# Batch 2's local q and k: from transposes on TensorE to DMA transposes with ordering copies on VectorE

## The chip, the cores and the metric

One core of a Trainium2 chip runs the kernel. The metric is the time of one execution on the device, in microseconds; a run's time is compared with runs of the kernel before. Engines are named as in the profile: PE (TensorE), DVE (VectorE), ACT (ScalarE), POOL (GpSimd) and SP (SyncE, which here only issues DMAs). DMAs are issued by POOL (loads from memory, which also change float32 to bfloat16) and by SP (stores and DMA transposes).

## The reference

Eight batches, eight heads, 576 positions, head size 64. Heads 0 to 3 attend locally (the last 32 positions), heads 4 to 7 attend to positions at a stride of 32. The attention's output feeds a two-layer network with a squared relu:

```python
scores = scale * np.matmul(q, k.transpose(0, 1, 3, 2))
mask_local = (rel >= 0) & (rel < stride)
mask_strided = (rel >= 0) & (pos[None, :] % stride == pos[:, None] % stride)
...
attn = softmax over the masked scores; attn_out = np.matmul(attn, v)
x = attn_out.transpose(0, 2, 1, 3).reshape(B * S, H * D)
h = x @ w_in          # 4608 x 512 by 512 x 2048
g = np.maximum(h, 0.0) ** 2
out = g @ w_out       # 4608 x 2048 by 2048 x 512
```

## The kernel before

The network is computed in nine chunks of 512 tokens. A chunk has 16 groups of the first product (`mm1`, line 848: four matmuls each, then a relu on ACT into one of four buffers `r`, then one step later a square on DVE into `g`) and 16 groups of the second (`mm2`, line 951: four matmuls each; after every fourth group of an output tile ACT copies the result and SP stores it). All groups are numbered 0 to 287 and put out in order; groups 32 to 47 are chunk 1's first product, 48 to 63 its second one, and group 64 is the first that needs batch 2's attention output. The last two chunks (`SEVEN`) replace the second product by seven smaller products of sums (`mm2_7`, line 915), for which `squares` (line 889) makes sums of the squares on DVE and a copy on POOL. In these two chunks the tiles of the first product come in the order 0, 8, 1, 9, ... 7, 15, and the sums for tile ff are made when ff is 8 or more.

The attention of the batches is woven between these groups. The table `PLAN` says ahead of which group a step is put out: the line `38: C3k G2+0+1+2+4+5+6` puts these steps ahead of group 38. There is no other planner: every engine and every queue executes what it is given in the order in which the program puts it out, so a step's place in the table is its place on every engine that it uses. A helper `later(n, fn)` puts work out n groups later.

Heads are handled in pairs; a pair of one batch is a "unit". Units 8 and 9 are the local pairs of batch 2, units 12 and 13 those of batch 3. The steps that the change touches:

- `l2k8+9`, `l2q8+9` (line 287): POOL loads k or q of both units, six positions to a row, into a part of `xt` that is still free. They stand in groups 6 and 12 and stay there.
- `c8kv` (line 300): a cast step, a reordering copy of unit 8's k on DVE from that place into a tile `k_l` of 96 rows.
- `T8kv` (line 487): six transposes on PE of 96x96 into a PSUM bank, then one copy on DVE (last letter `v`) or ACT (`a`) that evicts and puts the positions in order, into `kTl` (k) or `qT` (q).
- `A12k` (line 390): one DMA transpose, issued by SP, of the tile `k_l` into a spare part: for k, two further on among the four `kTl` buffers; for q, a tile `qT`.
- `R12kv` (line 397): a copy on DVE or ACT that puts the positions in order, from that spare part to `kTl` or a new `qT`. `A` and `R` together do what `T` does; batch 3 uses them already.
- `X2k`, `X2q` (line 358): DMA transposes of the strided heads' k and q, issued by SP. `C3k`, `C3q` (line 352): POOL loads the next batch's, into the tiles that X2k and X2q read.
- `G2+0+1+2+4+5+6` (line 580): local scores of units 8 and 9: 24 matmuls, unit 8's twelve first, into six PSUM banks; ACT takes exponentials of each bank (the numbers are the groups by which each is put off), DVE multiplies with the mask.
- `D8.0`, `D8.1` (line 807): exponentials times v for the first and second head of unit 8, then a division on DVE; `E8` (line 825): a DMA transpose, issued by SP, of unit 8's output into `xt`, which `mm1` reads.
- `H2v` (line 448): a copy on DVE of parts of v; `U3` (line 417): loads of v; `s2`, `x2+3` (lines 672, 700): scores and output of the strided heads; `k21v` (line 367): a copy on DVE of their k; `x1.0` to `x1.2` and `E5a`: the end of batch 1.

Of the kernel before, what the change touches and what calls it, by code (L numbers as in the profile page):

```python
# [40 lines left out]
21: s1.1 D5.0  # L41
22: l3k12+13 s1.2 U2
23: E4a D5.1
24: x1.0
26: X2k l3q12+13 x1.1 X2q
28: E5a x1.2
29: c8kv
30: c8qv
31: c9kv c9qv
33: T8kv  # L50
34: C3q T8qv
35: T9qa
36: H2v T9kv
38: C3k G2+0+1+2+4+5+6
39: c12kv A12k
40: c13kv A13k
43: D8.0
44: c12qv A12q
45: k21v c13qv A13q D9.0
47: U3 D8.1  # L60
48: Q16k D9.1 E8
49: E9
50: Q17q Q16q s2
52: Q17k
55: X3k X3q
56: C4k C4q x2+3
# [73 lines left out]
def kernel(  # L140
# [332 lines left out]
    def later(n, fn, key=None):  # L473
        pending.append((clock[0] + n, key, fn))
# [369 lines left out]
    gs = {}  # L844
# [3 lines left out]
    def mm1(c, ff, kks=range(4), order=range(4), pool=None):  # L848
        if c not in gs:
            gs[c] = g_pool.tile([128, 16, 512], BF16, name="g_sb")  # L850
        g = gs[c]
        if kks[0] == order[0]:
            phs[ff] = bank(pool or "ph")
        ph = phs[ff]
        for kk in kks:
            nc.tensor.matmul(ph, w_in_tile(kk, ff),  # L856
                             xt[kk][:, 512 * c:512 * (c + 1)],
                             start=(kk == order[0]), stop=(kk == order[-1]))
        if kks[-1] != order[-1]:
            return  # L860
        r = r_pool.tile([128, 512], BF16, name="r")
        nc.scalar.activation(r, ph, AF.Relu)  # L862
        if c in SEVEN:
            later(1, lambda: squares(c, ff, r))
            return
        later(1, lambda: nc.vector.tensor_tensor(g[:, ff, :], r, r, op=ALU.mult))  # L866
# [20 lines left out]
        nc.vector.tensor_tensor(t[nm], x, y, op=ALU.subtract)  # L887

    def squares(c, ff, r):
        g, i = gs[c], ff % 8  # L890
        if not ss:
            att.close()
            late = ctx.enter_context(tc.tile_pool(name="sums", bufs=1, reuse_waits="tile"))
            for nm in ("1", "2", "3", "4", "a"):
                ss[nm] = late.tile([128, 8, 2, 128], mybir.dt.float32r, name=f"s{nm}")
        nc.vector.tensor_tensor(g[:, ff, :], r, r, op=ALU.mult)  # L896
        if ff < 8:
            return
        S = {k: x[:, i] for k, x in ss.items()}
        a1, a2 = (g[:, k, :].rearrange("p (u t c) -> p u t c", u=2, t=2) for k in (i, ff))  # L900
        nc.gpsimd.tensor_copy(S["a"], a2[:, :, 1])  # L901
        nc.vector.tensor_tensor(S["1"], a1[:, :, 1], a2[:, :, 1], op=ALU.add)
        nc.vector.tensor_tensor(S["2"], S["1"], a1[:, :, 0], op=ALU.subtract)
        last = lambda: nc.vector.tensor_tensor(S["4"], a2[:, :, 0], S["2"], op=ALU.subtract)
        later(15 + (4, 4, 5, 6, 7, 8, 9, 10)[i] - 2 * i, last)
        if i < 7:
            return
        for k in range(0, 8, 4):
            a1 = g[:, k:k + 4, :].rearrange("p k (u t c) -> p (k u) t c", u=2, t=2)
            nc.vector.tensor_tensor(ss["3"][:, k:k + 4].rearrange("p k u c -> p (k u) c"), a1[:, :, 0], a1[:, :, 1],  # L910
                                    op=ALU.subtract)
# [298 lines left out]
```

## Time and profile before

| | us |
|---|---|
| median of three runs | 295.23 (294.79 to 295.24) |
| the profiled execution | 295.08 |
| its span, first to last instruction | 293.4 |
| PE busy | 287.2 (98%) |
| DVE busy | 199.9 (68%) |
| ACT busy | 167.0 (57%) |
| POOL busy | 86.7 (30%) |

Rows of the order of instructions give the start in us from the span's start, the length in us, the engine, the line, the operation, output <- input, the shape, and in brackets how long the engine sat idle before and what ended that. SPq and POOLq are the engines' queues of DMA issues; the length of such a row is the length of the issue, not of the transfer. Rows of the chain of waits give start, length, and the work on the chain that ended last. Rows of DMA issues end with the time from issue to landing. PEld is the loading of weights into PE, which overlaps the matmuls.

### The profile page before, as it was taken

The page shows a single profiled execution, that of the slowest core. Times are in us where ns is not written, and L with a number is a line of the kernel's source. Part 1 is how long each engine was busy: PE and PEld are TensorE (multiplying, and loading weights), DVE is VectorE, ACT ScalarE, POOL GpSimd, SP SyncE. Part 2 cuts the span into 40 slices and gives each one's busy share as a digit, 9 for nine tenths or more (in the row PEclk, how much of TensorE's full clock was granted, in tenths as well). Part 3 has the DMA queues.
Part 4 walks back from the last instruction along what each step waited for, and adds up shares of the span by engine and source line. Part 5 has one row for each costly group of instructions (what it writes and reads, how often), then busy time and mean ns, then how long its engine had stood idle before and what let it go on. Part 6 is the DMA issues. An engine that isn't in the chain of part 4 may idle for free.

```text
span 293.4 us, 6453 instructions
## 1 busy us (share of the span) xinstructions
PE 287.2 (98%) x2506; PEld 152.5 (52%) x2506; DVE 199.9 (68%) x489; ACT 167.0 (57%) x306; POOL 86.7 (30%) x135
## 2 busy tenths in 40 slices
PE   7999999999999999999999999999999999999995
PEld 3554555544444454544445444444444444984594
DVE  5666797776366746866366826673389979968983
ACT  3767846674657644764567446654676367306610
POOL 8974552062343047074303720000000013102300
PEclk9999999999999999999999999999999999999999
DMA  7999999999999999999998997411001200020003
GB/s 151 180 210 207 199 201 181 171 246 107 185 218 165 129 190 212 152 135 179 179 141 115 178 169 147 84 56 74 36 22 38 93 36 0 2 107 37 2 1 143
DMA packets 91470, 37.23 MB, mean 127 GB/s; under 512 B 77668, under 2 KB 84226, under 8 KB 91440
## 3 DMA queue, kind: packets, MB, share of 16 engines
q0 software_dynamic: 50352, 18.14, 55.6%
q1 hardware_dynamic: 40944, 18.62, 31.2%
q8 instruction: 19, 0.31, 0.4%
q14 instruction: 11, 0.09, 0.1%
q10 hardware_dynamic: 144, 0.07, 0.1%
HBM read 36.83 MB, written 9.44 MB: 158 GB/s over the span
## 4 chain that ended last, share of the span: by engine, by line
PE 96%; DMA 2%; DVE 0%; issue 0%; DVEq 0%; POOLq 0%
PE psb L856 43%; PE psb L962 33%; PE psb L932 9%; DMA w_out_b<-in_q_dram 2%; PE psb L815 2%; PE psb L589 1%; PE psb L544 1%; PE psb L492 1%; PE psb L743 1%; PE psb L680 1%; PE psb L748 1%; PE psb L514 1%; PE psb L337 0%; PE psb L837 0%; PE psb L327 0%
## 5 line engine op out<-in xcount | busy, mean ns | idle before, releaser
L856 PE MATMUL psb<-xt,w_in 128*128 128x512 bf16 x576 | 131.6, 379 | 0.0
L862 ACT ACTIVATE r<-psb 128x512 bf16<-128x512 f32 x144 | 85.6, 599 | 45.6 <-PE psb L856 42.5
L962 PE MATMUL psb<-w_out_b,g_sb 128*128 128x512 bf16 x448 | 101.0, 379 | 0.0
L856 PEld LDWEIGHTS <-w_in 128*128 128x128 bf16 x576 | 53.8, 98 | 60.3 <-issue 0.5
L866 DVE TENSOR_TENSOR g_sb<-r 128x512 bf16<-128x512 bf16 x112 | 47.0, 423 | 43.8 <-ACT r L862 42.6
L962 PEld LDWEIGHTS <-g_sb 128*128 128x128 bf16 x448 | 42.0, 98 | 47.6
L966 ACT COPY y<-psb 128x512 f32<-128x512 f32 x28 | 16.5, 589 | 42.6 <-PE psb L962 42.5
L901 POOL CAST sa<-g_sb 128x256 fp32r<-128x256 bf16 x16 | 9.7, 603 | 98.1 <-DVE g_sb L896 98.1
L725 DVE TENSOR_TENSOR xt<-psb,rv 64x288 bf16<-64x288 f32 x36 | 17.3, 479 | 14.3 <-ACT rv L713 13.9
L599 ACT ACTIVATE e<-psb 128x384 bf16<-128x384 f32 x36 | 15.5, 505 | 2.8 <-PE psb L589 2.8
L821 DVE TENSOR_TENSOR x_l<-psb,rinv 96x384 bf16<-96x384 f32 x28 | 15.5, 554 | 1.0
L596 DVE TENSOR_TENSOR e<-e,mask_all 128x576 bf16<-128x576 bf16 x24 | 10.0, 454 | 8.8 <-ACT e L599 8.6
L896 DVE TENSOR_TENSOR g_sb<-r 128x512 bf16<-128x512 bf16 x32 | 13.0, 419 | 3.3 <-ACT r L862 3.3
L355 POOL DMA_DIRECT2D q_t<-in_q_dram x6 | 3.4, 568 | 38.0 <-DMA qT_s<-q_t 35.9
L284 POOL DMA_DIRECT2D q_l<-in_q_dram x16 | 11.6, 729 | 8.1 <-DMA v_s<-in_v_dram 3.7
L284 POOL DMA_DIRECT2D k_l<-in_k_dram x16 | 11.7, 735 | 1.7 <-issue 0.9
L932 PE MATMUL psb<-t,s 128*128 128x256 f32 x96 | 12.2, 283 | 0.0
L718 DVE TENSOR_TENSOR xt<-psb,rv 64x162 bf16<-64x162 f32 x24 | 11.2, 469 | 1.2 <-ACT rv L713 0.5
L932 PEld LDWEIGHTS psb<-t,s 128*128 128x128 f32 x96 | 11.6, 189 | 0.0
L355 POOL DMA_DIRECT2D k_t<-in_k_dram x6 | 3.2, 536 | 27.3 <-DMA kT_s<-k_t 25.9
L944 DVE TENSOR_TENSOR y<-psb,y 128x256 f32<-128x256 f32 x19 | 8.0, 423 | 4.3 <-PE psb L932 3.5
L443 POOL DMA_DIRECT2D vl<-in_v_dram x8 | 9.8, 1226 | 3.8 <-DVE xt L718 2.9
(153 smaller groups left out, 303.4 us busy)
## 6 DMA issues: line engine op xcount, KB each, us to landing
out_dram<-y SPq DMA_DIRECT2D x35, 256.0 KB, 2.7
vl<-in_v_dram POOLq DMA_DIRECT2D x8, 288.0 KB, 8.2
w_out_b<-in_moe_w_out_dram POOLq DMA_DIRECT2D x4, 512.0 KB, 14.7
q_t<-in_q_dram POOLq DMA_DIRECT2D x7, 288.0 KB, 6.3
k_t<-in_k_dram POOLq DMA_DIRECT2D x7, 288.0 KB, 7.2
w_in<-in_moe_w_in_dram POOLq DMA_DIRECT2D x2, 768.0 KB, 13.5
v_s<-in_v_dram POOLq DMA_DIRECT2D x12, 108.0 KB, 7.7
k_l<-in_k_dram POOLq DMA_DIRECT2D x16, 72.0 KB, 7.5
```

The source lines that it names most:

```text
L284: nc.gpsimd.dma_start(out=t[:, :, hh, :], in_=src[b, 2 * p + hh].rearrange("(t p) d -> p t d", p=QL))
L599: nc.scalar.activation(e[:, row, 4 * QL * i:4 * QL * (i + 1)], bk[row][i][:, 0:4 * QL], AF.Exp, scale=scale)
L718: nc.vector.tensor_tensor(t, po[half(par), f].rearrange("c (a g m) -> c g m a", a=n, g=3), rv[half(par), w * f:w * (f + 1)].rearrange("c ( ...
L725: nc.vector.tensor_tensor(to[:, :, :, :, par], po[half(par)].rearrange("c f (a h m) -> c h m f a", a=n, h=3)[:, h], rv[half(par)].rearrang ...
L821: nc.vector.tensor_tensor(x, po[0:QL, :, 0:D], rinv[0:QL].to_broadcast([QL, NL, D]), op=ALU.mult)
L856: nc.tensor.matmul(ph, w_in_tile(kk, ff), xt[kk][:, 512 * c:512 * (c + 1)], start=(kk == order[0]), stop=(kk == order[-1]))
L862: nc.scalar.activation(r, ph, AF.Relu)
L866: later(1, lambda: nc.vector.tensor_tensor(g[:, ff, :], r, r, op=ALU.mult))
L896: nc.vector.tensor_tensor(g[:, ff, :], r, r, op=ALU.mult)
L932: nc.tensor.matmul(pa, a, b, start=k == 0 and n not in "273", stop=k == 7, skip_group_check=True)
L962: nc.tensor.matmul(py, g[:, ff, 128 * j:128 * (j + 1)], w_out_b[:, ff, :], start=(ff == 0), stop=(ff == 15))
L966: nc.scalar.copy(y, py)
```

## The change

Two parts. First, `T8kv`, `T8qv`, `T9qa` and `T9kv` (24 transposes on PE, three evictions on DVE and one on ACT) go. In their place stand `A8k`, `A9k`, `A8q`, `A9q` (four DMA transposes on SP) and `R8kv`, `R9kv`, `R8qv`, `R9qv` (four ordering copies on DVE). The casts move from groups 29 to 31 to groups 24 (k) and 28 (q), directly ahead of their DMA transposes; X2k and X2q move from group 26 to 29, so that on SP they stand behind the four new transposes. G2 moves from group 38 to 40, D8.0 from 43 to 44, D9.0 from 45 to 46, D8.1 from 47 to 48, D9.1 from 48 to 49, E9 from 49 to 50; E8 follows D9.1, from 48 to 49.

Second, in the two `SEVEN` chunks the sums for ff 14, until now put out directly behind its square, are put out two groups later, by a new function `sums`: behind the square of ff 7 and ahead of that of ff 15. The last difference of ff 14 (`last`) keeps its place.

```diff
-24: x1.0
-26: X2k l3q12+13 x1.1 X2q
-28: E5a x1.2
-29: c8kv
-30: c8qv
-31: c9kv c9qv
-33: T8kv
-34: C3q T8qv
-35: T9qa
-36: H2v T9kv
-38: C3k G2+0+1+2+4+5+6
-39: c12kv A12k
-40: c13kv A13k
-43: D8.0
-44: c12qv A12q
-45: k21v c13qv A13q D9.0
-47: U3 D8.1
-48: Q16k D9.1 E8
-49: E9
-50: Q17q Q16q s2
+24: c8kv c9kv A8k A9k x1.0
+26: l3q12+13 x1.1
+28: E5a x1.2 c8qv c9qv A8q A9q
+29: X2k X2q
+34: C3q
+35: R8kv
+36: H2v R9kv
+38: C3k R8qv
+39: c12kv A12k R9qv
+40: c13kv A13k G2+0+1+2+4+5+6
+44: c12qv A12q D8.0
+45: k21v c13qv A13q
+46: D9.0
+47: U3
+48: Q16k D8.1
+49: D9.1 E8
+50: Q17q Q16q s2 E9
...
     def squares(c, ff, r):
...
         nc.vector.tensor_tensor(g[:, ff, :], r, r, op=ALU.mult)
-        if ff < 8:
-            return
+        if ff == 14:
+            later(2, lambda: sums(g, ff))
+        elif ff > 7:
+            sums(g, ff)
+
+    def sums(g, ff):
+        i = ff % 8
         S = {k: x[:, i] for k, x in ss.items()}
         a1, a2 = (g[:, k, :].rearrange("p (u t c) -> p u t c", u=2, t=2) for k in (i, ff))
         nc.gpsimd.tensor_copy(S["a"], a2[:, :, 1])
         nc.vector.tensor_tensor(S["1"], a1[:, :, 1], a2[:, :, 1], op=ALU.add)
         nc.vector.tensor_tensor(S["2"], S["1"], a1[:, :, 0], op=ALU.subtract)
         last = lambda: nc.vector.tensor_tensor(S["4"], a2[:, :, 0], S["2"], op=ALU.subtract)
-        later(15 + (4, 4, 5, 6, 7, 8, 9, 10)[i] - 2 * i, last)
+        later(15 + (4, 4, 5, 6, 7, 8, 7, 10)[i] - 2 * i, last)
```

More of the change, by code (lines that the diff above doesn't have):

```diff
@@ L889, in squares @@
     def squares(c, ff, r):
-        g, i = gs[c], ff % 8
+        g = gs[c]
         if not ss:
```

## The prediction

> **What bounds the kernel now.** I read the page, then the chain of waits, then the order of instructions on VectorE (DVE) and on the queues around the change, then the issues of DMAs. The page first:
>
> ```profile
> PE 287.2 (98%) x2506; PEld 152.5 (52%) x2506; DVE 199.9 (68%) x489; ACT 167.0 (57%) x306; POOL 86.7 (30%) x135
> DMA  7999999999999999999998997411001200020003
> PE 96%; DMA 2%; DVE 0%; issue 0%; DVEq 0%; POOLq 0%
> ```
>
> TensorE (PE) carries 96% of the chain, so anything taken off PE shortens the run, and any wait put before it lengthens it by its whole length. The DMA engines have no free slice until two thirds of the span. The chain at the place of the change (start, length, work; "L492 x6" is one of the four steps of transposes on PE that go, the first and the last of them shown, "L589 x24" the local scores of batch 2):
>
> ```profile
> 52.38 0.26 PE psb L492 x6
> 52.64 0.86 PE psb L856 x4
> ...
> 55.74 0.26 PE psb L492 x6
> 57.73 0.77 PE psb L589 x24
> 58.50 4.42 PE psb L856 x20
> ...
> 83.22 6.91 PE psb L856 x32
> ...
> 97.63 0.62 PE psb L589 x24
> ```
>
> PE runs without a hole. A group of the large matmuls takes 0.86. The scores take 0.77 here and 0.62 for batch 4: the first lost 0.15 to T9kv, whose eviction ends at 58.02 (DVE row 57.28 below).
>
> **What goes.** Four times 0.26 of PE transposes: 1.04 us. Nothing else hides there, so all of it is gain. Their evictions (three on DVE, one on ScalarE) go too.
>
> **What comes, on DVE.** Four ordering copies (L404), all on DVE, in groups 35, 36, 38 and 39, and the scores G2 only two groups later than before, in group 40. These rows price them:
>
> ```profile
> 50.76 0.36 DVE L303 COPY k_l<-xt 96x768 bf16<-96x768 bf16 x1
> 51.04 0.35 DVE L303 COPY q_l<-xt 96x768 bf16<-96x768 bf16 x1
> 53.05 0.42 DVE L866 TENSOR_TENSOR g_sb<-r 128x512 bf16<-128x512 bf16 x1 [1.12 <-ACT r L862]
> 56.87 0.48 DVE L450 COPY vl<-vl 32x1280 bf16<-32x1280 bf16 x1
> 57.28 0.74 DVE L499 COPY kTl<-psb 128x576 bf16<-128x576 bf16 x1
> L404 DVE COPY kTl<-kTl x1: 648/648/648, 80.9 to 80.9; 128x576 bf16<-128x576 bf16 x1
> ```
>
> Back to back, each starts 0.08 before the last ends (50.76 + 0.36 against 51.04), so a square costs 0.34 in a row, a copy 0.57, H2v 0.40, a cast 0.27. The square of the group that ended at 52.38 started at 53.05: it is ready 0.67 after its group. Without the transposes groups 33 to 39 end at 53.24, 54.11, 54.97, 55.84, 56.70, 57.56 and 58.43, where G2 should start. DVE in its order: square 34 to 55.20; R8kv 55.12; square 35 from 55.69; H2v 56.03; R9kv 56.43; square 36 from 57.00; square 37, ready at 57.37; R8qv from 57.7; square 38 58.3; c12kv 58.6; R9qv from 58.9 to 59.55. The second half of G2 (unit 9) needs R9qv and would be due at 58.74. So with every transfer in time G2 still ends at about 59.6 + 0.31 = 59.9, or 59.97 with the chain's 0.06 of lag. Before, the same point (G2 done, two groups more done) is 58.50 + 1.73 = 60.23. Gain so far 0.26, of the 1.19 that transposes and T9kv's wait would give.
>
> **What comes, on the DMA queues.** Four DMA transposes of 96x768 on SP: A8k, A9k behind casts in group 24, A8q, A9q behind casts in group 28, and all ahead of X2k and X2q. They are issued in the stretch where the engines are full. Issues there (start, length of issue) and, from the list of DMA issues in short stretches, us to landing:
>
> ```profile
> 43.38 0.64 POOL L426 DMA_DIRECT2D v_s<-in_v_dram  x1 [0.96 <-DMA xt<-in_k_dram]
> 48.98 0.70 POOL L296 DMA_DIRECT2D xt<-in_q_dram  x1 [0.84 <-DMA q_t<-in_q_dram]
> 50.20 2.31 SPq L360 DMA_TRANSPOSE kT_s<-k_t  x1
> 52.56 5.16 SPq L360 DMA_TRANSPOSE qT_s<-q_t  x1
> 60.41 0.53 POOL L355 DMA_DIRECT2D q_t<-in_q_dram  x1 [10.73 <-DMA qT_s<-q_t]
> v_s<-in_v_dram POOLq DMA_DIRECT2D x1, 40.5 KB, 10.9
> xt<-in_q_dram POOLq DMA_DIRECT2D x1, 288.0 KB, 9.1
> kT_s<-k_t SPq DMA_TRANSPOSE x1, 8.6
> qT_s<-q_t SPq DMA_TRANSPOSE x1, 7.3
> DMA to landing us min/median/max: 8.9/10.7/11.5
> qT<-q_l SPq DMA_TRANSPOSE x1, 5.8
> ```
>
> The load of 48.98 lands at 58.1; X2k, issued after it on another queue, lands at 50.20 + 8.6 = 58.8, X2q at 59.9. Though SP's queue was empty, X2k came home just behind the last load issued before it. I read from this that transfers land about in order of issue over both queues. X2q follows X2k by 1.06 (80x2048); 96x768 has 45% of that, 0.48.
>
> A8k and A9k are issued at about 44.3 and 45.5 (the k load is in by then: the v_s load's wait for it ended at 43.38). The load of 43.38 lands at 54.3, so A8k lands near 55 and A9k near 56.5: R8kv is due at 55.1, R9kv at 56.4, so little is lost. The load of 48.98 is pushed by 2 x 0.48 to 59.0. A8q is issued at 51.12, where a cast ends today: it lands at 59.5, in 8.4 us, and A9q at 60.0. Bounds: the four transposes of this shape in the next full stretch, A12 and A13 (line 393, the row of min/median/max), took 8.9 to 11.5; the last row, a transpose of 96x768 issued at 93.9, took 5.8. I take 8.4, nearest to X2k in the same place.
>
> Then R8qv waits on DVE from 57.7 to 59.5. Behind it stand square 38, c12kv, R9qv and squares 39 on; ScalarE has four r buffers, enough for this wait, so the loss arises at G2: R8qv 59.5, square 38 60.07, c12kv 60.42, R9qv 60.7 to 61.35, unit 9 from 61.4, G2 done at 61.77. Against 60.23 that is a loss of 1.54, transposes already counted.
>
> **Small steps.** D8.0 stands four groups behind G2, not five. Its sixth block reads columns that the second mask writes:
>
> ```profile
> 60.87 0.49 ACT L599 ACTIVATE e<-psb 128x384 bf16<-128x384 f32 x1
> 61.35 0.35 DVE L303 COPY k_l<-xt 96x768 bf16<-96x768 bf16 x1
> 61.62 0.82 DVE L596 TENSOR_TENSOR e<-e,mask_all 128x576 bf16<-128x576 bf16 x2
> 65.25 0.82 DVE L596 TENSOR_TENSOR e<-e,mask_all 128x576 bf16<-128x576 bf16 x2
> ```
>
> The masks end 3.94 behind G2's end, and 3.68 once c13kv's cast is out of the way; four groups are 3.46, and the sixth block comes 0.15 later. Loss 0.1 to 0.4; I take 0.2. For D8.1 the masks end 7.57 behind, 7.2 without a cast, against 7.3: nothing, bound 0.3. D9.0 and D9.1 read the same two masks two groups and one group later: nothing. The moved casts c8kv, c9kv cost 0.6 of DVE around 44, c8qv and c9qv take the place of today's: nothing on PE. X2k and X2q stand behind four transposes of 0.48, so X2q lands near 62, not at 59.9; POOL's wait at 60.41 (C3q, which overwrites what X2q reads, and the loads behind it) grows by 2 us. The four stores of chunk 0 and A12k, A13k behind X2q on SP go out as much later; chunk 1 needs the y buffers only from group 51 on, R12k comes in group 57: nothing. What these feed (X3, then s3 at 90, and E9 issued near 72 for group 64 at 83.22) has 4 us of room or more: nothing, and up to 2 us if not.
>
> The late sums:
>
> ```profile
> 248.89 0.60 ACT L862 ACTIVATE r<-psb 128x512 bf16<-128x512 f32 x1 [0.27 <-PE psb L856]
> 249.57 0.50 DVE L903 TENSOR_TENSOR s<-s,g_sb 128x256 fp32r<-128x256 f32 x1
> 250.00 0.81 DVE L896 TENSOR_TENSOR g_sb<-r 128x512 bf16<-128x512 bf16 x2
> 250.46 1.53 PEld L932 LDWEIGHTS <-g_sb 128*128 128x128 bf16 x15 [0.27 <-DVE g_sb L896]
> 251.72 2.35 DVE L910 TENSOR_TENSOR s<-g_sb 128x1024 fp32r<-128x1024 bf16 x2
> 254.41 0.42 DVE L944 TENSOR_TENSOR y<-psb,y 128x256 f32<-128x256 f32 x1 [0.35 <-issue]
> ```
>
> Today the square of ff 7 runs at 250.00, behind the two sums of ff 14 (the second at 249.57), and the weight load for it waits 0.27, of which some 0.15 reach PE (0.27 less the 0.11 between loads). Afterwards it runs at 249.52, when its relu is done (248.89 + 0.60): that wait goes, 0.15 in each of two chunks. But DVE idles 0.44 from 249.08, so the long differences end at 254.5 and the first y sum starts 0.14 late, on which the next products wait some 0.1. Bounds per chunk: gain 0.15, loss 0.3 (0.44 less the 0.15). I take a gain of 0.07, together 0.15.
>
> **Sum.** +1.54 (transposes, copies, landing) + 0.2 (D8.0) - 0.15 (sums) = +1.6. The profiled execution took 295.08 (span 293.4), 0.15 under the median of 295.23: 295.08 + 1.6 = 296.7. Within 0.2% is what this kernel's measurement can hardly tell from no change: 294.64 to 295.82.
>
> **Rivals.** *Transfers take turns.* If the queues are served by turns, a transpose needn't wait for older loads: with the 5.8 of the last row, issued with loads still out, A8q lands at 56.9, A9q near 58.2, both before DVE gets to them. Then -0.26 + 0.2 - 0.15 = -0.2: 294.9. For it: that row, and the 5.8 was in a full slice too. Against: X2k, the rows of 8.9 to 11.5, all of one order with the loads. The Trainium skill, page "DMA: Bandwidth & Descriptors", section "Queues, rings and completion order", says that each DMA engine goes round between the queues that have work, a packet at a time; by that rule this rival, 294.9, is the outcome and not 296.7. The trace, with X2k 0.7 behind the load's landing, speaks for order of issue instead.
>
> *Faster: PE at G2 doesn't wait at all.* If transfers are in time and DVE gets its copies done ahead of squares that come late, by 58.7, the full 1.19 stays, with 0.3 of the sums: 293.6. It decides at R9qv's end, 58.7 against my 59.55. Against it: DVE's rows leave no 0.85 there.
>
> *Much slower: landings as in the next stretch.* With 11.4 for A8q and 11.5 for A9q (issued 52.4) R9qv starts at 63.9, G2 ends at 65.0: +4.7 + 0.2 - 0.15, 299.8. For it: same shape and queue. Against: there new loads were issued alongside; here POOL stands still, waiting for X2q. A late E9 would cost up to 2 beside the forecast, 298.7.
>
> **How the numbers follow.** Forecast, with A8q landing in 7.5 to 10 us, each us worth one (295.8 to 298.2): 0.58. By turns, 294.6 to 295.8: 0.22. No wait at G2: 0.10. Much slower, or E9: 0.10. The range leaves out the ends of these: 294.7 to 298.2; the likeliest one's own is 295.8 to 298.2. Faster 0.10, same 0.22, slower 0.68.
>
> **What would show it.** In the changed profile: no L492 after 50 us; L404 four times on DVE before 62 at 0.65; A8q's issue at 51.1 with 8 us to landing; the scores L589 with a hole before their second half of 2 to 3 us, put down to qT's copy or transfer; X2q landing near 62; 249.5 for the square of ff 7 and no wait of 0.27. I am wrong if A8q and A9q land within 6.5 us, if DVE gets to R9qv before 58.5, or if a later stage (E9 before 83) waits.

## The result, and the profile after

| | before | after |
|---|---|---|
| median, us | 295.24 (294.79 to 298.14) | 302.58 (300.95 to 303.5) |
| ratio, 95% interval | | 1.0239 [1.0213, 1.0266] |
| profiled execution, us | 295.08 | 302.43 |
| its span, us | 293.4 | 300.7 |

The change makes the kernel 2.4% slower, 7.35 us by the two profiled executions. Executions more than 1.5% above the fastest of the same kernel are left out of the ratios, here and below, but not of the medians. Lines of the kernel shift by a few: after, L401 are the ordering copies, L390 the DMA transposes, L586 the local scores, L593 their masks, L677 the strided scores, L853 and L964 the two products, L812 exponentials times v, L934 the smaller products; in the experiments they lie within a few lines of these. The page of the kernel after, busy time of PE, granted clock by slice, and the shares of the chain:

```profile
PE 288.3 (96%) x2482; PEld 152.1 (51%) x2482; DVE 200.3 (67%) x490; ACT 166.9 (56%) x305; POOL 86.5 (29%) x135
PEclk9999999969999999999999999999999999999999
PE 90%; DMA 6%; DVE 2%; issue 1%; ACT 0%; POOL 0%; DVEq 0%; POOLq 0%
```

DMA has 6% of the chain where it had 2%, and the ninth slice (60 to 67.7 us) has a clock of 0.6. PE executes 24 instructions fewer and is busy 1.1 us longer: work that was taken away, and more time. The chain of the kernel after shows where:

```profile
52.24 11.24 DMA qT<-q_l
...
63.51 0.66 DVE qT L401
...
64.20 0.66 PE psb L586 x12
64.87 5.64 PE psb L853 x16
...
74.65 0.37 DVE e L593
...
77.55 0.37 PE psb L677 x32
...
91.06 6.91 PE psb L853 x32
...
284.42 13.06 PE psb L934 x112
```

And of the kernel before, the points that answer to the last rows:

```profile
69.70 0.37 PE psb L680 x32
...
276.67 13.14 PE psb L932 x112
```

With the points shown in the prediction the 7.35 come apart. G2 is done at 64.87 instead of 60.23: +4.64, the transposes' 1.04 already counted. The four groups 40 to 43 behind it take 5.64 instead of 3.46: +2.18 (with the holes filled, below, they take 3.57, so these parts are good to 0.1). From there to the strided scores s2 (77.55 against 69.70, 7.85 later) another 1.03 is lost, at D8.1. Group 64 starts 7.84 later (91.06 against 83.22), so batch 2's outputs E8 and E9 come in time. The products end at 297.48 instead of 289.81, 7.67 later, so the late sums gained 0.17. The rest, 0.3, comes back in the last stores. PE's own rows show the three holes, and DVE's what ended two of them:

```profile
61.37 0.43 PE L586 MATMUL psb<-qT,kTl 64*128 64x96 bf16 x12 [3.13 <-DVE qT L401]
64.20 0.66 PE L586 MATMUL psb<-qT,kTl 64*128 64x96 bf16 x12 [2.41 <-DVE qT L401]
75.07 0.57 PE L812 MATMUL psb<-vl,e 128*128 128x65 bf16 x6 [0.75 <-DVE e L593]
```

```profile
54.92 0.65 DVE L401 COPY kTl<-kTl 128x576 bf16<-128x576 bf16 x1
...
56.45 0.65 DVE L401 COPY kTl<-kTl 128x576 bf16<-128x576 bf16 x1
57.02 0.75 DVE L863 TENSOR_TENSOR g_sb<-r 128x512 bf16<-128x512 bf16 x2
60.67 0.64 DVE L401 COPY qT<-qT 128x576 bf16<-128x576 bf16 x1 [2.90 <-DMA qT<-q_l]
...
63.51 0.64 DVE L401 COPY qT<-qT 128x576 bf16<-128x576 bf16 x1 [1.60 <-DMA qT<-q_l]
```

DVE is where the prediction put it until 57.8; then it waits for A8q (landed 60.65) and, behind two more rows, for A9q (63.48). The DMA issues of the kernel after, one at a time (the last column is us from issue to landing): V2's load, issued at 39.56; A8k and A9k (44.01, 45.41); the load l3q (49.25); A8q (50.96). A9q is the first row of the chain.

```profile
vl<-in_v_dram POOLq DMA_DIRECT2D x1, 288.0 KB, 16.1
kTl<-k_l SPq DMA_TRANSPOSE x1, 8.9
kTl<-k_l SPq DMA_TRANSPOSE x1, 9.8
xt<-in_q_dram POOLq DMA_DIRECT2D x1, 288.0 KB, 13.6
qT<-q_l SPq DMA_TRANSPOSE x1, 9.7
```

So A8k landed at 52.95, ahead of V2, which was issued 4.5 us earlier and landed at 55.65; before, V2 landed in 12.3, at 51.98. And l3q, at 58.13 before, landed at 62.87.

### The profile page after: what moved, and what is told of

The parts are those of the page before. It is cut to its first block, busy times and chain, and to the rows that moved or that the text cites. A ratio compares the mean times of both kernels' runs of the same rounds, so it can differ in the third digit from the quotient of the medians.

```text
span 300.7 us, 6418 instructions
## 1 busy us (share of the span) xinstructions
PE 288.3 (96%) x2482; PEld 152.1 (51%) x2482; DVE 200.3 (67%) x490; ACT 166.9 (56%) x305; POOL 86.5 (29%) x135
## 4 chain that ended last, share of the span: by engine, by line
PE 90%; DMA 6%; DVE 2%; issue 1%; ACT 0%; POOL 0%; DVEq 0%; POOLq 0%
PE psb L853 39%; PE psb L964 33%; PE psb L934 9%; DMA qT<-q_l 4%; DMA w_out_b<-in_k_dram 2%; PE psb L812 2%; PE psb L586 1%; PE psb L541 1%; PE psb L740 1%; PE psb L677 1%; PE psb L745 1%; PE psb L489 1%; PE psb L511 0%; DVE g_sb L863 0%; PE psb L834 0%
## 5 line engine op out<-in xcount | busy, mean ns | idle before, releaser
L853 PE MATMUL psb<-xt,w_in 128*128 128x512 bf16 x576 | 132.9, 384 | 0.0
L964 PE MATMUL psb<-w_out_b,g_sb 128*128 128x512 bf16 x448 | 101.2, 379 | 0.0
L853 PEld LDWEIGHTS <-w_in 128*128 128x128 bf16 x576 | 54.6, 99 | 63.1 <-issue 3.1
L964 PEld LDWEIGHTS <-g_sb 128*128 128x128 bf16 x448 | 41.9, 98 | 47.4
L968 ACT COPY y<-psb 128x512 f32<-128x512 f32 x28 | 16.5, 589 | 42.6 <-PE psb L964 42.5
L593 DVE TENSOR_TENSOR e<-e,mask_all 128x576 bf16<-128x576 bf16 x24 | 10.0, 455 | 9.3 <-ACT e L596 9.1
L281 POOL DMA_DIRECT2D k_l<-in_k_dram x16 | 11.7, 735 | 3.7 <-DMA k_t<-in_k_dram 2.6
L934 PE MATMUL psb<-t,s 128*128 128x256 f32 x96 | 12.3, 285 | 0.0
L715 DVE TENSOR_TENSOR xt<-psb,rv 64x162 bf16<-64x162 f32 x24 | 11.2, 468 | 1.2 <-ACT rv L710 0.5
L934 PEld LDWEIGHTS psb<-t,s 128*128 128x128 f32 x96 | 11.8, 189 | 0.0
L812 PEld LDWEIGHTS <-e 128*128 128x128 bf16 x168 | 8.2, 97 | 6.2 <-DVE e L593 1.4
```

Source lines behind the costliest of these rows:

```text
L281: nc.gpsimd.dma_start(out=t[:, :, hh, :], in_=src[b, 2 * p + hh].rearrange("(t p) d -> p t d", p=QL))
L812: nc.tensor.matmul(po[:, n, :], e[:, c:c + 128], rhs[:, NL * part + n, 0:D + 1], start=True, stop=True)
L853: nc.tensor.matmul(ph, w_in_tile(kk, ff), xt[kk][:, 512 * c:512 * (c + 1)], start=(kk == order[0]), stop=(kk == order[-1]))
L934: nc.tensor.matmul(pa, a, b, start=k == 0 and n not in "273", stop=k == 7, skip_group_check=True)
L964: nc.tensor.matmul(py, g[:, ff, 128 * j:128 * (j + 1)], w_out_b[:, ff, :], start=(ff == 0), stop=(ff == 15))
L968: nc.scalar.copy(y, py)
```

## The experiments

Theory at the start: q is late (its landing), k is not. Rivals: the clock, the places of the other steps, the number of transposes. The first two runs take the parts of the change alone.

**Sums only.** The kernel before with `sums` put off for ff 14 (second half of the diff).

> The kernel before with the second part of the change alone (sums of ff 14 two groups later). My theory: the wait of 0.27 in front of the weight load of ff 7 goes in both chunks, and each chunk's seven products take 0.07 to 0.15 less: 0.15 to 0.3 less in all, 295.0. Rival: VectorE's 0.44 of idleness is handed on to the first sums of y and to the products behind them: no gain or up to 0.3 more.

294.74 (294.46 to 301.91), ratio 0.9986 [0.9975, 0.9996]. The second part is a small gain, 0.4 us, and none of the loss comes from it. This is the only version here that is shown to be faster than before.

**k only.** The kernel before with DMA transposes for k, PE transposes for q, G2 where it was, no sums:

```diff
-24: x1.0
+24: c8kv c9kv A8k A9k x1.0
-29: c8kv
-31: c9kv c9qv
+31: c9qv
-33: T8kv
+33: R8kv
-35: T9qa
-36: H2v T9kv
+35: R9kv T9qa
+36: H2v
```

> The kernel before with only k by DMA transposes (A8k, A9k in group 24, R8kv in 33, R9kv in 35), q still on TensorE, scores in group 38. Theory 1 (the loss comes from the q transposes landing behind the scores' place; the k ones land in time, near 53 and 55): two steps of transposes less on TensorE and no wait at the scores, 0.5 to 0.7 less than before, 294.6. Theory 2 (any DMA transposes put into the full stretch cost TensorE, since the loads of v and of batch 3 are pushed back by 4 us and VectorE waits for them): a wait at the scores or at H2v stays, 296 or more.

298.05, ratio 1.0088 [1.0065, 1.0111]. PE in order, the DMA rows of A9k (issued 46.33) and of l3q (issued 49.62), and the stretches 48 to 54 and 54 to 60 (the last columns are clock, DMA share and GB/s):

```profile
61.13 0.43 PE L588 MATMUL psb<-qT,kTl 64*128 64x96 bf16 x12 [2.84 <-DVE kTl L403]
```

```profile
kTl<-k_l SPq DMA_TRANSPOSE x1, 14.1
xt<-in_q_dram POOLq DMA_DIRECT2D x1, 288.0 KB, 17.2
```

```profile
48.00:54.00 6.00, 6.00 (x44) 3.06 (x42) 3.62 (x12) 4.29 (x9) 1.32 (x2) 1.00 2.56 95
54.00:60.00 6.00, 4.24 (x39) 2.06 (x36) 2.27 (x5) 3.89 (x7) 0.00 (x0) 1.00 1.85 114
```

The idea that k is in time falls: with only two transposes A9k took 14.1 us, and l3q landed at 66.79, 8.7 later than before. Before, 171 GB/s were moved from 48 to 54, and from 54 to 60:

```profile
54.00:60.00 6.00, 6.00 (x59) 3.09 (x58) 4.03 (x9) 3.92 (x8) 0.00 (x0) 1.00 1.25 204
```

**q only.** The places of the change, with A8q, A9q and their copies, but k transposed on PE and the sums as before; the difference from the changed kernel, without the lines of the sums:

```diff
-24: c8kv c9kv A8k A9k x1.0
+24: x1.0
-29: X2k X2q
+29: X2k X2q c8kv c9kv
+33: T8kv
-35: R8kv
-36: H2v R9kv
+36: H2v T9kv
```

> The changed plan with only q by DMA transposes (A8q, A9q in group 28, R8qv, R9qv in 38 and 39, scores in 40), k still on TensorE, the sums as before. Theory 1a (the k transposes ahead push the loads, and with them the q transposes, by 3 to 4 us): without them A8q lands near 57, A9q near 59, the scores wait 1.5 us or less, the clock stays, 295 to 296.5. Theory 1b (the q transposes are late by the loads in front of them and by their own turn, whatever the k ones do): A8q near 60, A9q near 62, the two holes and the low clock stay, 299 to 301.

296.92, ratio 1.0056 [1.0036, 1.0076]. PE in order, then the DMA rows of l3q (issued 49.97), A8q (51.13) and A9q (52.52):

```profile
59.85 0.43 PE L586 MATMUL psb<-qT,kTl 64*128 64x96 bf16 x12 [0.99 <-DVE qT L401]
61.00 0.43 PE L586 MATMUL psb<-qT,kTl 64*128 64x96 bf16 x12 [0.72 <-DVE qT L401]
...
69.50 0.57 PE L812 MATMUL psb<-vl,e 128*128 128x65 bf16 x6 [0.50 <-DVE e L593]
```

```profile
xt<-in_q_dram POOLq DMA_DIRECT2D x1, 288.0 KB, 9.2
qT<-q_l SPq DMA_TRANSPOSE x1, 8.0
qT<-q_l SPq DMA_TRANSPOSE x1, 7.1
```

Here A8q and A9q land at 59.13 and 59.65, close to the 59.5 and 60.0 of my prediction; for the whole change they were 60.65 and 63.48. D8.0 is stretched by 0.19 (0.53 against D9.0's 0.34), as predicted; D8.1 waits, at a clock of 1.00.

**Holes filled.** The changed kernel with 14 and 11 more matmuls of 512 columns ahead of unit 8's and unit 9's scores (into the bank that the scores overwrite), so that PE has something to do in the holes:

```diff
+    FILL = (14, 11)
...
+            if b == 2 and t % NL == 0:
+                for _ in range(FILL[t // NL]):
+                    nc.tensor.matmul(bk[0][2], w_out_b[:, 0, 0:128], w_out_b[:, 0, :], start=True, stop=True)
```

> The changed kernel with matmuls for nothing put into the two holes at the scores: 14 ahead of unit 8's and 11 ahead of unit 9's (512 columns each, into a bank that the scores overwrite). It computes the same. Theory: the granted clock of 0.5 after the holes comes from TensorE's standing idle; with the holes filled groups 40 to 43 take 3.46 instead of 5.64, and the time is about 2.2 less than the changed kernel's, 300.2. Rival: the clock falls for another reason (the transfers, the burst behind the holes): 302.4 or more.

301.22 (299.91 to 302.3), ratio 1.0204 [1.0169, 1.0239]. The chain of this kernel, and the clock of the kernel after in the same stretch (its column is the 1.00 or 0.50 ahead of the last two):

```profile
65.19 3.57 PE psb L858 x16
```

```profile
64.00:66.00 2.00, 1.79 (x15) 0.88 (x15) 0.75 (x3) 0.00 (x0) 0.00 (x0) 0.50 1.22 312
66.00:68.00 2.00, 2.00 (x6) 0.73 (x5) 0.43 (x1) 0.98 (x2) 1.49 (x3) 0.50 1.06 332
68.00:70.00 2.00, 2.00 (x8) 0.78 (x7) 0.94 (x3) 1.31 (x3) 1.86 (x4) 0.74 0.97 89
```

With PE kept busy the groups 40 to 43 take 3.57, not 5.64: the clock had fallen because PE stood idle. All four executions have a mean clock of 1.000; the changed kernel's six have 0.972 to 0.994. G2 was done 0.32 later (65.19), and of the 2.1 saved 1.8 remain between the profiled executions, 1.4 between the medians; the intervals of the two ratios overlap, so the times alone leave this gain open; the clocks don't. D8.1 still waited, 0.56 us.

**Loads behind.** The changed kernel with two load steps moved out of the stretch, behind C3q, which waits for X2q; what reads l3q's data moves with it:

```diff
-22: l3k12+13 s1.2 U2
+22: l3k12+13 s1.2
-26: l3q12+13 x1.1
+26: x1.1
-34: C3q
+34: C3q U2 l3q12+13
-44: c12qv A12q D8.0
-45: k21v c13qv A13q
+44: D8.0
+45: k21v
-52: Q17k
+52: Q17k c12qv A12q
+53: c13qv A13q
-58: V4 R12qa
+58: V4
+60: R12qa
```

> The changed kernel with batch 2's loads of v (U2) and batch 3's load of q (l3q) put out behind C3q, so that on POOL they wait until X2q has landed; batch 3's casts and DMA transposes of q move to groups 52 and 53, R12qa to 60. Theory (loads and transposes that are in flight together slow each other, 115 to 145 GB/s in such stretches against 200 for loads alone and 260 for transposes alone, and so push each other's landing): A8q lands by 57.5 and A9q by 59, the scores wait less than 1 us, the clock stays at 1.00, 294.5 to 296. Rival (the four transposes are slow by themselves in this stretch): A8q 60 or later, A9q 62 or later, holes and low clock stay, 300 or more.

296.09 (295.45 to 300.0), ratio 1.0037 [1.0005, 1.0069]: 6.5 of the 7.3 us come back, with all four transposes still there. PE in order, and the transfer on its chain ahead of them:

```profile
59.43 0.43 PE L588 MATMUL psb<-qT,kTl 64*128 64x96 bf16 x12 [0.64 <-DVE qT L403]
60.59 0.43 PE L588 MATMUL psb<-qT,kTl 64*128 64x96 bf16 x12 [0.72 <-DVE qT L403]
```

```profile
45.95 11.53 DMA kTl<-k_l
```

A8q and A9q landed 6.7 and 5.9 us after issue, at 58.20 and 58.70: they had waited for these loads. The transposes of k are no quicker for it. A9k took 11.53 where it took 9.77 in the changed kernel, and V2's load, issued ahead of both, took 16.5 us as there (16.1), not the 12.3 of the kernel before. So what the two transposes of k cost the older loads does not come from the loads that were moved.

**All four behind the last load.** The same number of transposes, the k ones 7 us later:

```diff
-24: c8kv c9kv A8k A9k x1.0
+24: x1.0
-28: E5a x1.2 c8qv c9qv A8q A9q
+28: E5a x1.2 c8kv c8qv A8k A8q c9kv c9qv A9k A9q
-35: R8kv
-36: H2v R9kv
-38: C3k R8qv
-39: c12kv A12k R9qv
+36: H2v
+38: C3k R8kv R8qv
+39: c12kv A12k R9kv R9qv
```

> The changed kernel with all four casts and transposes in group 28, behind the issue of l3q, in the order A8k, A8q, A9k, A9q, and the ordering copies R8kv, R8qv ahead of group 38 and R9kv, R9qv ahead of group 39; all else as in the change. The same number of transposes of the same size, only the k ones some 7 us later. Theory (a transpose is dear where it goes in among loads that are still under way, as the k ones of group 24 do; behind the last load it costs 0.5 us): l3q lands as before, 58 to 60, the four at about 59.1, 59.7, 60.2 and 60.8, one hole of about 2 us before unit 8 and one of 1 to 1.5 us before unit 9, G2 done near 62.6, no fall of the clock, D8.1 up to 0.5 late: 297.9, from 297 to 299. Rival (what counts is how many transposes are under way before R9q's, wherever they stand): A9q lands at 63 or later, G2 is done at 64.5 or later and the clock falls: 301 to 303.

299.06 (298.19 to 301.16), ratio 1.0114 [1.009, 1.0138]; its profiled execution is the longest, 301.16. DMA rows of l3q (issued 50.06) and A8k (51.75), then PE in order, and clocks (the clock is the figure ahead of the last two):

```profile
xt<-in_q_dram POOLq DMA_DIRECT2D x1, 288.0 KB, 9.8
kTl<-k_l SPq DMA_TRANSPOSE x1, 8.0
```

```profile
61.12 0.58 PE L585 MATMUL psb<-qT,kTl 64*128 64x96 bf16 x12 [2.15 <-DVE qT L400]
62.83 0.67 PE L585 MATMUL psb<-qT,kTl 64*128 64x96 bf16 x12 [1.12 <-DVE qT L400]
```

```profile
61.10:61.40 0.30, 0.28 (x11) 0.27 (x11) 0.30 (x2) 0.00 (x0) 0.00 (x0) 0.78 1.12 437
61.40:61.80 0.40, 0.30 (x8) 0.09 (x3) 0.40 (x3) 0.26 (x1) 0.00 (x0) 0.50 1.14 256
```

The four landed at 59.79, 60.41, 60.94 and 61.42, about half a microsecond apart, together with l3q and behind it (59.83): nearly the spacing that I had taken for the change. So transposes of the same size that are cheap when they are issued behind the last load are dear when k's go out in group 24. The time is higher than the theory's 297.9: in the profiled execution G2 was done at 63.49, not at 62.6, and the clock fell here too, which the theory had not foreseen. The one execution whose mean clock was 0.999 took 298.19. X2q, the last of the stretch, landed at 65.4, hardly earlier than in the changed kernel (66.0): the place of the transposes decided who waits, not when all is done.

**Scores late.** The changed kernel with G2 in group 47, behind every landing, and the steps behind it later, E8 and E9 in groups 56 and 57:

```diff
...
-40: c13kv A13k G2+0+1+2+4+5+6
...
+40: c13kv A13k
...
+47: U3 G2+0+1+2+4+5+6
...
-49: D9.1 E8
-50: Q17q Q16q s2 E9
...
+56: D9.1 E8
+57: V3 R12kv E9 X3k X3q
```

> The changed kernel with the scores G2 in group 47 instead of 40, R8qv and R9qv in 44 and 45, D8 and D9 in 51 to 56, E8 in 56, E9 in 57, s2 in 54, x2 in 60; all transposes and loads are put out as in the changed kernel until X2q. Theory (the whole loss comes from the scores standing ahead of the landings at 60.7 and 63.5: the holes, the low clock behind them, and the backlog that makes D8.1 wait): no hole at the scores, clock 1.00, 294 to 295.5, unless E9 now lands behind group 64, which costs up to 1.5. Rival (the transfers slow TensorE in another way): 299 or more.

303.45, ratio 1.0287 [1.0256, 1.0318]: a miss for the expectation that this would mend it. Unit 8's scores no longer wait, unit 9's still do for 1.18, and three holes opened at group 64. PE in order, and a row of the chain that ends in the third hole:

```profile
85.13 0.39 PE L856 MATMUL psb<-xt,w_in 128*128 128x512 bf16 x1 [0.83 <-DMA xt<-x_l]
88.21 0.60 PE L856 MATMUL psb<-xt,w_in 128*128 128x512 bf16 x2 [2.68 <-DMA xt<-x_l]
90.13 2.29 PE L856 MATMUL psb<-xt,w_in 128*128 128x512 bf16 x5 [1.32 <-DVE xt L718]
```

```profile
69.38 11.62 DMA qT<-q_l
```

The first two holes end in the landing of E8 and E9. The third ends in the strided heads' output on DVE, which was late because ACT, ahead of its part in it, had waited 3.70 in R12qa for A12q (landed 81.00); the strided heads' steps had been moved back as well. So E8 and E9 come too late for group 64 when they are issued in groups 56 and 57, but they are not the only ones, and the run doesn't tell what they alone would cost. From 89 to 95 the clock stood at 0.50 here too.

**q only, D8.1 later.** The q-only kernel with D8.1 in group 49, D9.1 and E8 in 50, E9 in 51.

> The kernel with only q by DMA transposes and D8.1, D9.1, E8, E9 one group later each. Theory (D8.1's wait for the second masks is VectorE's backlog behind the late copies, 0.75 in that run's D8.1): it goes, 0.5 to 0.9 less than the 296.9 of q alone, 296.2. Rival (the backlog only moves on to the next step): 296.9.

295.96, ratio 1.0034 [1.0012, 1.0057]: 0.96 less than q only by the medians, though the intervals overlap, and PE has one hole left up to group 64, before unit 9's scores:

```profile
61.48 0.43 PE L587 MATMUL psb<-qT,kTl 64*128 64x96 bf16 x12 [0.73 <-DVE qT L402]
```

In this execution DVE waits for no transfer at all, and R9qv still runs only from 60.79: the 0.73 is the length of DVE's own queue in front of G2. The wait at D8.1 was the same engine's work ahead of the second masks; one group of room took it away.

**k only, loads behind.** The k-only kernel with the load steps moved as above.

> The kernel with only k by DMA transposes, with U2 and l3q behind C3q as above (casts and transposes of batch 3's q in 52 and 53, R12qa in 60). Theory (mixing): A9k no longer takes 14 us, lands before 57, the scores do not wait for it, 294.3 to 295. Rival (k's transposes are late by the loads issued before them, V2 and l3k, alone): A9k near 60, 298.

297.62, ratio 1.0084 [1.0054, 1.0114]. The hole before the scores shrank from 2.84 to 0.59, but a new one of 1.95 opened at 86.37: ACT waited 2.89 in R12qa for A12q, which the moved loads had made late. A9k took 11.7 us and landed at 57.68, neither before 57 nor near 60 as the two expectations had it. So the total says little; the hole at the scores is the part that bears on the question.

**k transposes that nobody uses.** The kernel before, with casts and A8k, A9k issued in group 24 beside the PE transposes that stay:

```diff
-24: x1.0
+24: c8kv c9kv A8k A9k x1.0
-29: c8kv
-31: c9kv c9qv
+31: c9qv
```

> The kernel before with the two k transposes A8k and A9k (and their casts) issued in group 24, as in the change, but nobody reads what they bring: TensorE still transposes units 8 and 9 itself, so no wait for A8k or A9k exists. Theory (transposes and loads under way together move little; the delay is the transfers', and it costs time only through who waits for it): A8k and A9k land 9 to 14 us after their issue, l3q and X2q land some 4 us later than before (l3q at 62 to 64 where it was 58.1), and since X2q is needed only in the fifties of the groups the time hardly moves: 295.2, from 294.9 to 295.8. Rival (the loads pushed by transposes stop TensorE by themselves, through the third chunk's loads or the scores' loads X2): 296.3 to 298, with a hole of TensorE that ends in a load. Second rival (two more casts and two issues in the engines' queues cost time themselves): also slower, but with holes that end in ScalarE's or VectorE's work.

297.09 (294.42 to 301.52), ratio 1.0035 [0.9999, 1.007]: unclear. Four of twelve executions lie between 294.42 and 294.9, as if the transposes cost nothing; the others lie higher, up to 301.52. In the profiled one (300.81, the second longest) l3q took 16.0 us to land, V2's load 18.2, and H2v, which waits for V2 on DVE, stopped T9kv's eviction behind it for a hole of 1.80 before the scores. A second hole, 2.10 at 94.01, ended in the landing of the next batch's strided q (`qT_s`). That the pushed transfers alone can stop PE is seen there; one long execution doesn't explain the median, so how often, and what it costs, stays open.

**Loads behind, G2 in group 42 and in group 41.** Two attempts to remove the two holes that "loads behind" has left; D8 to E9 move along.

```diff
-40: c13kv A13k G2+0+1+2+4+5+6
+40: c13kv A13k
+42: G2+0+1+2+4+5+6
...
-49: D9.1 E8
-50: Q17q Q16q s2 E9
...
+52: Q17k D9.1 E8
+53: E9
+54: c12qv A12q
+55: c13qv A13q
```

> The changed kernel with U2 and l3q behind C3q (as in the experiment with the loads behind) and G2 at group 42 instead of 40, the D8 and D9 steps, E8 and E9 moved by two to four groups with it, the q of units 12 and 13 two groups later. With the loads behind, the changed kernel still had two holes before the scores of units 8 and 9, 0.64 and 0.72 us, and one of 0.3 us before D8.1; two groups of TensorE's work are 1.73 us, more than both holes together. Theory (what is left of the loss are these three holes): the holes go, 296.09 - 1.66 = 294.4, from 294.0 to 294.9, which is 0.15% to 0.4% faster than before. Rival (the wait only moves to E8 and E9, three and four groups later here, as in the experiment with the scores late): 295.2 to 297, with holes at group 64.

> As the run beside it, with G2 at group 41, one group (0.87 us) later than in the change. Theory: the hole before unit 8 goes and that before unit 9 shrinks to 0.0 to 0.5 us: 296.09 - 0.9 - 0.3 = 294.9, from 294.5 to 295.3. Rival (E8 and E9 late): E9 is one group earlier than in the run beside it, so the holes at group 64 would be smaller here than there.

295.83 with G2 in group 42, ratio 1.0028 [1.0004, 1.0052]; 295.45 in group 41, ratio 1.0011 [0.9985, 1.0038]. Neither beats the kernel before, and both lie above what was expected (294.0 to 294.9, and 294.5 to 295.3). In the profiled execution of the first (299.25, one of its longest) the holes were still there, 0.92 and 0.72, since DVE had stood 1.97 in H2v for V2's load and 0.59 in R9kv for A9k first; one of 2.62 at 87.20 came from ACT waiting 3.55 for A12q, not from E8 or E9 as the rival had it. In that of the second the holes before the scores were 0.31 and 0.71.

## Why the prediction was wrong in its size

The sign was right, and so was the place: DVE's copies of q, waiting for A8q and A9q, in front of G2. I said +1.6 us and it was +7.35. Point by point:

- *What goes*: no L492 at units 8 and 9, and the transposes' 1.04 lie inside the 4.64 by which G2 came late. Right.
- *DVE's order*: R8kv at 54.92 (said 55.12), R9kv 56.45 (56.43), the squares at 57.02 (57.00), DVE at R8qv from 57.8 (57.7). Right to 0.2. That G2 would gain 0.26 with every transfer in time was never run: nearest is the run with the loads behind, where DVE waited only 0.49, for A9k, and G2 was done at 61.02, later than the 60.23 of the kernel before and not earlier.
- *Landing*: the step that failed. I let A8k and A9k push the load of l3q by "2 x 0.48", to 59.0; they pushed it by 4.7, to 62.87, and A9q landed at 63.48, not at 60.0. The 0.48 was X2q's landing behind X2k's, scaled: a spacing of transposes that follow one another when the loads are over. As such it holds, to 0.15, in the run with all four behind the last load. It is not the price of a transpose that goes in between loads. That R8kv and R9kv were in time was luck: I had A8k near 55 and A9k near 56.5, behind the older loads, and they landed at 52.95 and 55.18 because they overtook them. The rows that I quoted as an upper bound, 8.9 to 11.5 for A12 and A13, were the right ones: 8.9, 9.8, 9.7 and 11.2 came. I set them aside with "there new loads were issued alongside", but three loads are issued alongside here as well, at 45.97, 47.78 and 49.25.
- *The rival "much slower"*, 299.8, had that landing: A8q 11.4, A9q 11.5, a loss of 4.7 at G2. A9q's 11.24 and the 4.64 measured are its numbers (A8q took 9.7). It missed the two terms that follow.
- *The clock*: a term that I had nowhere, 2.18. Holes were priced by their length alone. The runs show that the fall is a consequence of the holes: with them filled, 3.57 for the four groups and a mean clock of 1.000 in every execution.
- *D8.1*: "nothing, bound 0.3"; it lost 1.03, three times the bound. I measured how far behind G2 the second masks end in the kernel before, and left out what changes places with them. They are put out seven groups behind G2, so they moved from group 45 to 47. `k21v` and unit 13's cast of q stay in 45, and D9.0 moved by one group only, to 46. Before, these three ran on DVE behind the second masks (from 66.32; the masks started at 65.25). After, they stand ahead of them on the chain, with 0.16, 0.27 and, with its reciprocal, 0.67 for D9.0's division, 1.1 together:

```profile
73.19 0.16 DVE kc L373
73.35 0.27 DVE q_l L300
...
74.09 0.55 DVE x_l L818
```

  It doesn't take the slow clock: D8.1 waits 0.50 in q only and 0.56 with the holes filled, both at 1.00, and 0.30 with the loads behind, where the two casts of q stand later. Moving it one group later took the wait away in the q-only kernel.
- *D8.0*: 0.2 said; 0.19 of stretch in the q-only kernel; nothing in the changed kernel, whose four groups behind G2 were slow.
- *X2q*: said near 62, landed at 65.96. *E9*: 4 us of room or more, and no wait at group 64. Right, but with the scores late, E9 seven groups later still, PE waited for it there, though not for it alone.
- *Sums*: 0.15 said; 0.17 by the chain, 0.4 [0.1, 0.7] by the run with sums only.

*Transfers take turns*, the rival that would have given 294.9, was right in its mechanism where it matters least: A8k overtook V2, issued 4.5 us ahead of it. The Trainium skill, page "DMA: Bandwidth & Descriptors", section "Queues, rings and completion order", has the DMA engines go round the queues that have work; A8k's 52.95 against V2's 55.65 agrees. In group 28 no overtaking is seen: with q only, A8q landed at 59.13 together with l3q (59.15), issued 1.2 us ahead of it, so neither order of issue nor turns tells all landings here. What the rival got wrong is who pays: V2, l3q and all loads in between came 3.7 to 4.8 us later, and q's transposes behind them with them.

What is shown: that A9q's landing at 63.48 takes both k's transposes in group 24 and the two load steps (without the first it lands at 59.65, with them behind the last load at 61.42, without the load steps at 58.70), that the clock falls because of the holes, and that the place of the transposes decides who waits. What is only read from the rates is that k's transposes among loads move less in sum: 95 to 145 GB/s from 48 to 60 in the changed kernel and with k only, 162 with q only, 171 to 204 before. What in the DMA engines makes it so was not tried; that any transpose does it is not shown, since the kernel before had X2k and X2q beside its last loads at 204. No version with DMA transposes was shown to be faster than the kernel before.

## What to carry to other kernels

Price a transfer by rows of the same kind with the same company, and not by the spacing of transfers that run alone. A transpose on an engine that the trace shows as full can still be the cheaper one: 0.26 us of PE was replaced by 8.9 to 11.2 us from issue to landing on DMA engines that had no free slice, for no gain. Price a hole on PE by its length and by the clock behind it. And when a step moves, look for the work that is put off from it, and for what now stands ahead of that on its engine.

## What the runs showed of the hardware

- Two DMA transposes of 96x768, issued among loads, delayed a load issued after them by 4.7 us in the changed kernel and by 8.7 us with k only; issued behind the last load, four of them landed 0.5 to 0.6 us apart. A load issued ahead of the two took 16.5 us instead of 12.3 even in the run without the later loads.
- The clock's fall doesn't follow the length of a single hole. It stayed at 1.00 over a hole of 2.84 us (k only). With all four transposes behind the last load it fell during unit 8's scores, at about 61.25, after a hole of 2.15. In the changed kernel it was 1.00 for unit 8's scores, in spite of a hole of 3.13, and fell in the second hole. It came back only after some 5 us of work: PE worked from 64.20, and the stretch from 68 to 70 has a mean of 0.74.
- The Trainium skill, page "TensorE: Matmul & The Clock Gate", section "Why this matters for your kernels", advises no idle gaps of PE over some 3 us. The traces agree only in part: 2.84 left the clock alone, but 2.15 was enough elsewhere, and after 3.13 the scores still ran at 1.00. The same page, section "What's actually happening", says that the activity window is free-running, so that the moment of a change varies with where in it the work falls; no run here shows the window itself, but such a spread would follow from it.
